# Weight conversion in a linear attention and two-MoE kernel: whole 32-bit words instead of 16-bit halves between ScalarE and VectorE

## The chip, the cores and the metric

The kernel runs on one core of a Trainium2 chip. The metric is the time of one execution on the device in microseconds (us). The kernel before took 1602.63 us (median of three runs, 1600.29 to 1602.99). Durations below come from one more execution that was profiled.

Five engines work side by side, each through its own queue of instructions in order: TensorE (PE, with PEld for its weight loads), VectorE (DVE), ScalarE (ACT), GpSimd (POOL) and SyncE (SP), which here only issues DMA transfers.

## The reference

Everything is float32. A linear attention (8 batches, 8 heads, 576 positions, 64 per head) is followed by two feed-forward blocks over 4608 tokens of 512 features:

```python
q_s = softmax(q, axis=-1); k_s = softmax(k, axis=2)
kv = einsum('bhsd,bhse->bhde', k_s, v)
x = einsum('bhsd,bhde->bhse', q_s, kv)        # reshaped to 4608 x 512
g = x @ w_gate                                 # 512 x 1536
y = (silu(g) * (x @ w_val)) @ w_out            # 1536 x 512
h = maximum(maximum(y @ w1, y @ w2), y @ w3)   # each 512 x 768
out = h @ w_out2                               # 768 x 512
```

## The kernel before

The weights reach the kernel as 64-bit floats: a weight tile of 128 x 512 numbers lies in a staging buffer as 128 x 1024 32-bit words, where word 0 of each pair is the low half of the double and word 1 the high half. The kernel makes float32 numbers of them itself ("conversion"), with two instructions on ScalarE and two on VectorE for each tile:

- `convert_act`: L486 reads the high words (one word in two) as floats, drops the sign, scales by a power of two and writes the result into the resident weight tile `plain`. L487 reads the low words as integers, scales them so that the upper three bits remain, and writes them as 16-bit integers. Their place is the lower half of the **high** word, so that L487 writes where L486 reads.
- `convert_dve`: L495 masks the high word in place, so that its sign bit and the three new bits remain (one source, one constant). L498 shifts `plain` left by three and merges the masked word into it.

There are 60 weight tiles to convert (12 each of `G`, `V` and `O` for the first block, 6 each of `W1`, `W2`, `W3` and `P` for the second). Each is converted once, in the first of nine token blocks (j = 0, 512 tokens each). `G`, `V` and `W1` to `W3` then stay in SBUF. `O` and `P` are written to DRAM as float32 and read again by every later block.

The matmuls take each float32 operand as two parts, `hi` (rounded, by a cast on ScalarE, L513) and `lo` (the rest, by a subtraction on VectorE, L518), and form three products (`mm3`, L524). Six tiles (`WHOLE`) are used as plain float32 (L554).

The work goes in groups of one weight tile each: `G`, `V`, `O`, ... and then `W1`, `W2`, `W3`, `P`, ... The loop over groups writes every engine's queue by hand, in this order: `convert_dve` of tiles that ScalarE has begun, `split_lo` for the group three ahead, `split_hi` for the group four ahead (L513), `convert_act` by a quota (about six groups ahead), the group's matmuls, steps of the attention for the next token block (`SLOTS`), and then `main_ev`, which takes the result out of PSUM: Silu on ScalarE (`s`, L587) for `G`, a product on VectorE (`h`, L590) for `V`, a copy on ScalarE (L594) for `W1`. Two PSUM banks serve these results in turn. The third and fourth results of the first block (`G1`, `V1`) lie in banks `acc0` and `acc1`, so the first accumulating matmul (L554, tile `O0`) can start only when L587 has emptied `acc0`, and its second quarter only when L590 has emptied `acc1`. A prologue (`PROLOGUE`) does the first half of the attention and the first six conversions.

Staging buffers are filled by SP: seven tiles ahead at first, three ahead after the 34th, since the first phase borrows space (`ring_yhi`, `ring_ylo`) that later holds `y`.

Of the kernel before, what the change touches and what calls it, by code (L numbers as in the profile page):

```python
# [11 lines left out]
U16 = mybir.dt.uint16  # L12
AF = mybir.ActivationFunctionType
ALU = mybir.AluOpType
# [4 lines left out]
def linear_attention_moe_moe_kernel(  # L19
# [20 lines left out]
    nc = tc.nc  # L40
# [45 lines left out]
    n, m = R * HH * D, HH * D  # L86
# [357 lines left out]
    staged = {}  # L444
# [28 lines left out]
    def convert_act(n):  # L473

        j, kind, f = groups[n]
        if kind in "OP":
            plain[n] = sb.tile([128, TB], F32, tag="plain", name="plain", bufs=3)  # L480
        else:
            plain[n] = resident(kind, f)
        words = staged[n].rearrange("p (n t) -> p n t", t=2)
        low, high = words[:, :, 0], words[:, :, 1]
        bits = staged[n].bitcast(U16).rearrange("p (n t) -> p n t", t=4)[:, :, 2]
        nc.scalar.activation(out=plain[n], in_=high.bitcast(F32), func=AF.Abs, scale=2.0 ** -112)  # L486
        nc.scalar.activation(  # L487
            out=bits, in_=low, func=AF.Copy, scale=2.0 ** -29 * (1.0 - 2.0 ** -7), bias=-0.44
        )

    def convert_dve(n):
        j, kind, f = groups[n]
        rest = staged.pop(n).rearrange("p (n t) -> p n t", t=2)[:, :, 1]
        wu = plain[n].bitcast(U32)
        nc.vector.tensor_scalar(  # L495
            out=rest, in0=rest, scalar1=0x80000007, scalar2=None, op0=ALU.bitwise_and
        )
        nc.vector.scalar_tensor_tensor(  # L498
            out=wu, in0=wu, scalar=3, in1=rest, op0=ALU.logical_shift_left, op1=ALU.bitwise_or
        )  # L500
        if kind in "OP":
            nc.sync.dma_start(out=kept[kind][f * 128:(f + 1) * 128, :], in_=plain[n])

    def resident(kind, f):
        return raw[kind][:, f].rearrange("p c f -> p (c f)")
# [176 lines left out]
    def converts_act(upto):  # L682
        while done["act"] < min(upto, GPB):
            loads(done["act"] + 1)
            convert_act(order[done["act"]])
            done["act"] += 1

    def converts_dve(upto):
        while done["dve"] < min(upto, GPB):
            convert_dve(order[done["dve"]])  # L690
            done["dve"] += 1
            n = done["dve"]
            loads(n + 7 if n + 7 <= RING else max(RING, n + 3))
# [168 lines left out]
```

## Time and profile before

| What | Value |
|---|---|
| median of three runs | 1602.63 us |
| the profiled execution | 1602.22 us |
| its span, first to last instruction | 1600.3 us |
| PE busy | 1549.9 us (97% of the span) |
| DVE busy | 951.9 us (59%) |
| ACT busy | 740.6 us (46%) |
| mean granted TensorE clock | 0.992 of full speed |

PE is busy almost throughout, and the shares of DVE and ACT are means over nine blocks of which only the first converts weights. The slices of the page show this: ACT is busy 9 tenths of the third and fourth slices of 40 us and 3 to 4 tenths from the seventh slice on; PE has 3 and 7 tenths in the first two slices and 9 in all others. What PE still loses must be looked for in the first 240 us, stretch by stretch. "Busy" counts an instruction from its start to its end; two successive instructions of ACT or DVE overlap a little, so the pace of a queue is read from start to start.

### The profile page before, as it was taken

To read this page: it belongs to the slowest core of one execution; us is meant where nothing else is said; L and a number is where in the kernel's file an instruction comes from. 1 tells how busy PE (TensorE), PEld (TensorE's weight loads), DVE (VectorE), ACT (ScalarE), POOL (GpSimd) and SP (SyncE) were. 2 spreads that over 40 slices of the span, in tenths; PEclk is the share of its full clock that TensorE was granted. 3 is DMA by queue.
4 is the path that set the end of the run, shared out by engine and by line. 5 is a ranking of instruction groups with operands and counts; after the bars stand their busy time and mean duration, and the time that the engine had idled before them with its cause. 6 is when DMAs were issued, how large, how long until landed. Compare 5 with 4: busy or idle time off the path is not lost.

```text
span 1600.3 us, 19611 instructions
## 1 busy us (share of the span) xinstructions
PE 1549.9 (97%) x7300; PEld 1266.1 (79%) x7300; DVE 951.9 (59%) x1622; ACT 740.6 (46%) x1234; POOL 23.5 (1%) x33
## 2 busy tenths in 40 slices
PE   3799999999999999999999999999999999999999
PEld 2487678888888888888888888888888888888887
DVE  7687885457554765367546754575547643664443
ACT  3799864344434443354335443444343433443332
POOL 1000000000000000000000000000000000000000
PEclk9899999999999999999999999999999999999999
DMA  7674744102310322120412141123103211111100
GB/s 191 192 230 148 206 119 109 34 24 66 96 37 23 70 73 57 33 63 30 99 33 48 36 109 34 30 60 95 38 22 70 66 34 40 34 53 32 29 26 33
DMA packets 197182, 112.95 MB, mean 71 GB/s; under 512 B 145888, under 2 KB 169440, under 8 KB 197088
## 3 DMA queue, kind: packets, MB, share of 16 engines
q1 hardware_dynamic: 192288, 110.54, 25.6%
q10 hardware_dynamic: 4800, 1.18, 0.4%
q8 instruction: 57, 0.93, 0.3%
q14 instruction: 37, 0.30, 0.1%
HBM read 97.52 MB, written 14.16 MB: 70 GB/s over the span
## 4 chain that ended last, share of the span: by engine, by line
PE 86%; ACT 7%; DVE 4%; issue 2%; DMA 1%; SPq 0%; DVEq 0%; ACTq 0%
PE pm L524 58%; PE acc L524 25%; ACT stage L487 2%; ACT whi L513 1%; PE pkv L254 1%; PE acc L554 1%; PE px L407 1%; PE px L406 1%; PE px L405 1%; DMA out_dram<-o 0%; ACT raw_w L486 0%; SPq L148 0%; ACT plain L486 0%; ACT ring_yhi L487 0%; DVE wlo L518 0%
## 5 line engine op out<-in xcount | busy, mean ns | idle before, releaser
L524 PE MATMUL pm<-xhi,whi 128*128 128x512 f32 x864 | 339.6, 393 | 8.8 <-ACT s L587 4.8
L524 PE MATMUL pm<-xhi,wlo 128*128 128x512 f32 x864 | 337.5, 391 | 0.2 <-DVE wlo L518 0.2
L524 PE MATMUL pm<-xlo,whi 128*128 128x512 f32 x864 | 337.4, 390 | 0.0
L590 DVE TENSOR_TENSOR h<-s,pm 128x512 f32<-128x512 f32 x108 | 74.2, 687 | 334.3 <-PE pm L524 332.0
L524 PE MATMUL pm<-yhi,whi 128*128 128x512 f32 x648 | 255.2, 394 | 4.6 <-ACT s L594 4.3
L524 PE MATMUL pm<-ylo,whi 128*128 128x512 f32 x648 | 253.2, 391 | 0.2 <-DVE ylo L608 0.2
L524 PE MATMUL pm<-yhi,wlo 128*128 128x512 f32 x648 | 252.8, 390 | 0.0
L544 ACT CAST hhi<-h 128x512 fp32r<-128x512 f32 x156 | 97.3, 624 | 317.7 <-DVE h L590 209.7
L524 PEld LDWEIGHTS pm<-xhi,whi 128*128 128x128 f32 x864 | 162.8, 188 | 46.4 <-ACT s L587 6.9
L524 PEld LDWEIGHTS pm<-xhi,wlo 128*128 128x128 f32 x864 | 162.8, 188 | 35.3 <-DVE wlo L518 1.3
L524 PEld LDWEIGHTS pm<-xlo,whi 128*128 128x128 f32 x864 | 162.9, 189 | 34.1 <-issue 0.7
L524 PE MATMUL acc<-hhi,whi 128*128 128x512 f32 x424 | 165.0, 389 | 0.0
L524 PE MATMUL acc<-hhi,wlo 128*128 128x512 f32 x424 | 164.9, 389 | 0.0
L524 PE MATMUL acc<-hlo,whi 128*128 128x512 f32 x424 | 164.9, 389 | 0.0
L587 ACT ACTIVATE s<-pm 128x512 f32<-128x512 f32 x108 | 65.4, 605 | 180.7 <-PE pm L524 180.5
L524 PEld LDWEIGHTS pm<-yhi,whi 128*128 128x128 f32 x648 | 121.9, 188 | 33.3 <-ACT s L594 5.5
L524 PEld LDWEIGHTS pm<-yhi,wlo 128*128 128x128 f32 x648 | 122.1, 188 | 25.8
L524 PEld LDWEIGHTS pm<-ylo,whi 128*128 128x128 f32 x648 | 121.9, 188 | 25.2 <-DVE ylo L608 0.5
L513 ACT CAST whi<-raw_w 128x512 fp32r<-128x512 f32 x162 | 100.8, 622 | 56.5 <-PE pm L524 43.1
L518 DVE TENSOR_TENSOR wlo<-plain,whi 128x512 fp32r<-128x512 f32 x156 | 106.9, 685 | 17.1 <-ACT whi L513 17.0
L518 DVE TENSOR_TENSOR wlo<-raw_w,whi 128x512 fp32r<-128x512 f32 x162 | 109.9, 683 | 10.2 <-ACT whi L513 10.2
L545 DVE TENSOR_TENSOR hlo<-h,hhi 128x512 fp32r<-128x512 f32 x156 | 107.9, 692 | 12.5 <-ACT hhi L544 0.7
(149 smaller groups left out, 1959.1 us busy)
## 6 DMA issues: line engine op xcount, KB each, us to landing
plain<-kept_o SPq DMA_DIRECT2D x96, 256.0 KB, 2.6
plain<-kept_p SPq DMA_DIRECT2D x48, 256.0 KB, 2.8
out_dram<-o SPq DMA_DIRECT2D x36, 256.0 KB, 2.0
stage<-in_moe_w_dram SPq DMA_DIRECT2D x17, 512.0 KB, 3.9
k_sb<-in_k_dram SPq DMA_DIRECT2D x56, 128.0 KB, 3.3
v_sb<-in_v_dram SPq DMA_DIRECT2D x56, 128.0 KB, 2.8
stage<-in_moe_w_out_dram SPq DMA_DIRECT2D x12, 512.0 KB, 4.3
stage<-in_moe_w_gate_dram SPq DMA_DIRECT2D x6, 512.0 KB, 4.8
```

The lines of the kernel that those rows point to most:

```text
L254: nc.tensor.matmul(out=c["pkv"][u * D:(u + 1) * D, g, :], lhsT=lhsT, rhs=rhs, start=i == 0, stop=i == R,)
L405: nc.tensor.matmul(out=px[:, a:e], lhsT=hi, rhs=qhi, start=True, stop=False)
L406: nc.tensor.matmul(out=px[:, a:e], lhsT=hi, rhs=qlo, start=False, stop=False)
L407: nc.tensor.matmul(out=px[:, a:e], lhsT=lo, rhs=qhi, start=False, stop=True)
L487: nc.scalar.activation(out=bits, in_=low, func=AF.Copy, scale=2.0 ** -29 * (1.0 - 2.0 ** -7), bias=-0.44)
L513: nc.scalar.copy(out=hi, in_=plain[n])
L518: nc.vector.tensor_tensor(out=lo, in0=plain.pop(n), in1=hi, op=ALU.subtract)
L524: nc.tensor.matmul(out=o, lhsT=a, rhs=b, start=first and m == 0, stop=last and m == 2)
L544: nc.scalar.copy(out=hi, in_=h)
L545: later.append(lambda: nc.vector.tensor_tensor(out=lo, in0=h, in1=hi, op=ALU.subtract))
L587: nc.scalar.activation(out=st["s"], in_=p, func=AF.Silu)
L590: nc.vector.tensor_tensor(out=h, in0=st["s"], in1=p, op=ALU.mult)
```

## The change

L487 now writes its three bits as a whole 32-bit integer over the **low** word that it has read, and no longer as 16 bits into the high word. On VectorE the mask of one source becomes an operation with two sources: the high word is masked to its sign bit and merged with the low word in one instruction. The number of instructions on each engine stays the same, and so does their order. The new lines are one or two lines further up in the file (L486 becomes L484, L487 becomes L485, L495 becomes L494, L498 becomes L497, L513 becomes L512).

```diff
         words = staged[n].rearrange("p (n t) -> p n t", t=2)
         low, high = words[:, :, 0], words[:, :, 1]
-        bits = staged[n].bitcast(U16).rearrange("p (n t) -> p n t", t=4)[:, :, 2]
         nc.scalar.activation(out=plain[n], in_=high.bitcast(F32), func=AF.Abs, scale=2.0 ** -112)
         nc.scalar.activation(
-            out=bits, in_=low, func=AF.Copy, scale=2.0 ** -29 * (1.0 - 2.0 ** -7), bias=-0.44
+            out=low, in_=low, func=AF.Copy, scale=2.0 ** -29 * (1.0 - 2.0 ** -7), bias=-0.44
         )
 
     def convert_dve(n):
         j, kind, f = groups[n]
-        rest = staged.pop(n).rearrange("p (n t) -> p n t", t=2)[:, :, 1]
+        words = staged.pop(n).rearrange("p (n t) -> p n t", t=2)
+        low, rest = words[:, :, 0], words[:, :, 1]
         wu = plain[n].bitcast(U32)
-        nc.vector.tensor_scalar(
-            out=rest, in0=rest, scalar1=0x80000007, scalar2=None, op0=ALU.bitwise_and
+        nc.vector.scalar_tensor_tensor(
+            out=rest, in0=rest, scalar=0x80000000, in1=low, op0=ALU.bitwise_and, op1=ALU.bitwise_or
         )
```

What moves is a wait. On ScalarE's queue in the prologue, at the fourth to seventh conversions, the rows before stood as follows; `Activation_49` is the semaphore that ScalarE's own instructions raise, `DVE_49` and `PE_49` those of VectorE and TensorE, and `DMAHW` those of transfers:

```order
L486 ACTIVATE plain<-ring_yhi 128x512 [waits DMAHW6_49]
L487 ACTIVATE ring_yhi<-ring_yhi 128x512 [waits Activation_49]
L486 ACTIVATE raw_g<-ring_ylo 128x512 [waits DMAHW7_49]
L487 ACTIVATE ring_ylo<-ring_ylo 128x512 [waits Activation_49]
L486 ACTIVATE raw_v<-ring_ylo 128x512 [waits DMAHW0_49]
L487 ACTIVATE ring_ylo<-ring_ylo 128x512 [waits Activation_49]
```

And the same place in the changed kernel:

```order
L484 ACTIVATE plain<-ring_yhi 128x512 [waits DMAHW6_49]
L485 ACTIVATE ring_yhi<-ring_yhi 128x512
L484 ACTIVATE raw_g<-ring_ylo 128x512 [waits DMAHW7_49]
L485 ACTIVATE ring_ylo<-ring_ylo 128x512
L484 ACTIVATE raw_v<-ring_ylo 128x512 [waits DMAHW0_49]
L485 ACTIVATE ring_ylo<-ring_ylo 128x512
```

Before, all 60 instructions of L487 wait for the end of the L486 just ahead of them, because they write into words that it reads. In the changed kernel none does: 27 of the 60 still name ScalarE's own semaphore, but for an instruction at least eight places further back. VectorE's queue has one instruction replaced by another at each conversion, with the same waits.

## Rows read from the trace of the kernel before

**Rows 1.** Windows: us, busy us (count) of PE, PEld, DVE, ACT, POOL; PEclk, DMA share, GB/s

```profile
41.60:72.00 30.40, 21.98 (x57) 12.82 (x58) 17.98 (x31) 25.13 (x34) 0.00 (x0) 0.80 0.62 174
72.00:137.00 65.00, 65.00 (x286) 53.16 (x284) 52.28 (x94) 61.32 (x85) 1.15 (x1) 1.00 0.67 204
137.00:200.00 63.00, 57.01 (x251) 41.38 (x251) 48.33 (x86) 55.83 (x76) 1.28 (x1) 0.97 0.67 199
200.00:231.00 31.00, 28.24 (x142) 20.65 (x141) 26.19 (x49) 25.59 (x38) 0.00 (x0) 0.94 0.49 139
231.00:1600.30 1369.30, 1364.37 (x6464) 1129.15 (x6462) 777.98 (x1300) 557.51 (x982) 16.34 (x12) 1.00 0.20 51
```

**Rows 2.** Timeline of PE: start, us, instruction, [idle before, what ended it]

```profile
64.61 6.87 PE L554 MATMUL acc<-h,plain 128*128 128x512 f32 x8 [5.43 <-DVE stage L495]
...
149.11 0.67 PE L524 MATMUL pm<-xhi,whi 128*128 128x512 f32 x1 [3.39 <-ACT s L587]
...
178.85 0.50 PE L524 MATMUL pm<-yhi,whi 128*128 128x512 f32 x1 [1.51 <-ACT s L594]
...
223.41 0.50 PE L524 MATMUL pm<-yhi,whi 128*128 128x512 f32 x1 [1.98 <-ACT s L594]
```

**Rows 3.** Windows after three of those stalls: us, PE busy us (count), PEclk, DMA, GB/s

```profile
64.60:71.40 6.80, 6.79 (x9) 0.55 0.99 219
149.10:152.50 3.40, 3.39 (x8) 0.53 0.67 218
224.50:227.80 3.30, 3.30 (x9) 0.50 0.03 11
```

**Rows 4.** Timeline of ACT in the prologue: start, us, instruction

```profile
53.46 0.70 ACT L486 ACTIVATE raw_g<-ring_ylo 128x512 f32<-128x512 f32 x1
54.20 1.38 ACT L487 ACTIVATE ring_ylo<-ring_ylo 128x512 uint16<-128x512 uint32 x1
55.32 0.70 ACT L486 ACTIVATE raw_v<-ring_ylo 128x512 f32<-128x512 f32 x1
...
63.88 0.68 ACT L587 ACTIVATE s<-pm 128x512 f32<-128x512 f32 x1
64.46 0.60 ACT L513 CAST whi<-plain 128x512 fp32r<-128x512 f32 x1
```

**Rows 5.** Windows, instructions of L487 alone: us, ACT busy (count), PEclk, DMA, GB/s

```profile
51.00:65.00 14.00, 6.78 (x5) 0.96 0.61 191
72.00:137.00 65.00, 30.51 (x23) 1.00 0.67 204
```

**Rows 6.** Groups by line: shapes, xcount | busy us, mean ns of one | idle before

```profile
L487 ACT ACTIVATE stage<-stage 128x512 uint16<-128x512 uint32 x41 | 55.9, 1362 | 1.3
L486 ACT ACTIVATE raw_w<-stage 128x512 f32<-128x512 f32 x17 | 11.5, 679 | 2.1 <-DMA stage<-in_moe_w_dram 2.1
L495 DVE TENSOR_SCALAR stage<-stage 128x512 uint32<-128x512 uint32 x41 | 17.5, 427 | 20.6 <-ACT stage L487 20.4
L498 DVE SCALAR_TENSOR_TENSOR raw_w<-raw_w,stage 128x512 uint32<-128x512 uint32 x17 | 11.8, 693 | 0.6
L518 DVE TENSOR_TENSOR wlo<-raw_w,whi 128x512 fp32r<-128x512 f32 x162 | 109.9, 683 | 10.2 <-ACT whi L513 10.2
```

**Rows 7.** Timeline of DVE, two places: start, us, instruction

```profile
65.84 0.68 DVE L590 TENSOR_TENSOR h<-s,pm 128x512 f32<-128x512 f32 x1
...
103.51 0.68 DVE L590 TENSOR_TENSOR h<-s,pm 128x512 f32<-128x512 f32 x1
104.11 0.42 DVE L495 TENSOR_SCALAR stage<-stage 128x512 uint32<-128x512 uint32 x1
104.57 0.69 DVE L498 SCALAR_TENSOR_TENSOR raw_v<-raw_v,stage 128x512 uint32<-128x512 uint32 x1
```

**Rows 8.** Waits, of DVE (40 to 225 us) and ACT (60 to 225): us, times, longest

```profile
DVE stage L495 <- ACT stage L487: 18.3, 21, 2.1
ACT plain L486 <- DMA stage<-in_moe_w_out_dram: 4.5, 1, 4.5
```

## The prediction

> **What bounds the kernel now.** I read the windows by stretch first, since the shares of the whole span average nine token blocks of which only the first converts weights. From 231 us on PE is busy 1364.4 of 1369.3 us: nothing is to be had there. In the first block it lacks 8.4 us of 30.4 (41.6 to 72), nothing of 65 (72 to 137), 6.0 of 63 and 2.8 of 31 [rows 1]. So 17.2 us of idle time lie in reach of a change to the conversion; what PE lacks before 41.6 us is mostly softmax. The second view is PE's timeline at these stalls: 5.43 us before 64.61, 3.39 before 149.11, 1.51 before 178.85, 1.98 before 223.41, and three end on a ScalarE instruction that empties a PSUM bank [rows 2]. The first names L495, but the matmul there needs bank acc0, which L587 empties from 63.88 to 64.56, so it is ScalarE's too [rows 4]. Third, the clock after a stall: in the stretches after the first, second and fourth the granted clock is 0.55, 0.53 and 0.50, that is 1.2 GHz instead of 2.4 [rows 3]. A stall thus costs its idle time and then half of the stretch behind it: 3.4, 1.6 and 1.65 us.
>
> Who makes ScalarE late is seen in the same windows: ACT is busy 61.3 of 65 us and 55.8 of 63, DVE 52.3 and 48.3 [rows 1]. L487 has 30.5 us of the 61.3 [rows 5], at 1362 ns each where L486, of the same size, takes 679 [rows 6].
>
> **The change on ScalarE.** Today a conversion takes ACT's queue 1.86 us from start to start (53.46 to 55.32): 0.74 for L486, whose end L487 awaits, and 1.12 for L487 [rows 4]. Two things change. First the wait goes; the old L486 will overlap its successor as other instructions do, which follow each other after about 0.58 (63.88 to 64.46) [rows 4]. So 0.74 becomes 0.58. Second, L487 writes 32-bit words. The trace has no ScalarE instruction that writes every second word, so I bound its duration: not below 0.60 us, the cast L513 [rows 4], and not above the 1.36 us of today [rows 6]. L486 reads every second word, and differs from L487 in its output (packed words, not 16 bits in every fourth half-word) and in the input's type. I take L486's 0.68, the nearest row, as I put the excess on the 16-bit writes. Its pace is then 0.58 too. A conversion comes to 1.16 us and gives back 0.70; if only the wait goes, 0.16.
>
> **The change on VectorE.** L495 (427 ns, the next start 0.46 after its own: 104.11 to 104.57 [rows 7]) becomes an instruction with two sources. Below, it can't be faster than 427; the nearest row is L498, also with two sources, one of them every second word: 693 ns, against 683 for L518, whose operands all lie packed [rows 6]. A step of one word thus costs next to nothing in a read, and L495 reads and writes in such steps in 427. I take 0.69 and a step of 0.72 (L498 must still wait for its end): +0.26 per conversion. The upper bound is 1.36, the longest time that a conversion instruction has in these rows. With 23 conversions in 72 to 137 [rows 5] VectorE goes from 52.3 to 58.3 us of 65. It has that room: it stood waiting for L487 for 18.3 us at L495 alone [rows 8], and that wait shortens.
>
> Against this stands a rule of the Trainium skill (Vector Engine (DVE) Microarchitecture Reference, section 5.2, measured stream behaviour): a port keeps its full rate only for runs of at least two neighbouring words, and one that steps at every element takes 1.71 to 2.51 ns per column. By it the new instruction would take an estimated 0.95 to 1.36 us. The rows don't bear it out for a step of two words, since L495 takes 427 ns in just that pattern [rows 6]; it stays as the mechanism of a rival below.
>
> **The sum,** along the four stalls.
>
> - Up to 71.5 us. Two conversions of the prologue stand on the chain, each 0.70 less 0.26: -0.9. Between 51 and 65 us ScalarE does five conversions in a row [rows 5]: 5 x 0.70 = 3.5 of the 5.43 us stall. So L554 starts at 60.2 instead of 64.61. Its second quarter needs acc1, which L590 empties; L590 started 1.96 us after L587 (65.84 [rows 7] after 63.88), with VectorE's conversion and L518 between, and two conversions add 0.5. It starts at 59.5 + 1.96 + 0.5 = 62.0 and ends 0.68 later. Three quarters remain: 0.86 us each at full clock or 1.72 at half (6.87 for four [rows 2]). They end at 65.2 or 67.8 instead of 71.48: -6.3 or -3.7. The remaining idle time (about 1.9, then 1.6) is near that of the fourth stall, after which the half clock lasted 3.3 us and cost 1.65 [rows 3]; with that: -4.7.
> - 149.11: ScalarE is behind by what piled up since 72 us. 23 conversions x 0.70 = 16 us is far more than 3.39. The stall goes, and its 1.6 of half clock: -5.0.
> - 178.85: likewise, -1.5.
> - 223.41: the chain of waits behind it begins with a load of q for the next block, which needs a buffer that VectorE frees, and runs through 16 issues on SP's queue, the transfer and VectorE's maximum; two conversions are in it. The change moves these by about 1 us only. All of it would be -1.98 - 1.65 = -3.6; I take -2, with 0 and -3.6 as ends.
>
> Sum: -4.7 - 5.0 - 1.5 - 2.0 = -13.2. The profiled execution took 1602.22 (its span 1600.3 and 1.9 around it; the median of the runs is 1602.63, 0.4 more), so I forecast 1589.0. Ends of this case: -3.7 - 5.0 - 0 - 0 = -8.7 and -6.3 - 5.0 - 1.5 - 3.6 = -16.4, or 1585.8 to 1593.5. What the edits cost elsewhere is hidden by PE's own work: in 72 to 137 us it has no idle time at all [rows 1], and VectorE's extra 6 us run beside it.
>
> **Rivals.**
>
> (a) The write was not the cause. If L487 is slow through its stepped, in-place access or its integer input, only the wait goes. Five conversions give 0.8 where 5.43 are lost, and the prologue's two lose 0.1 each: -0.6, half clock as before. At 149.11, 23 x 0.16 = 3.7 still covers 3.39: -5.0. Nothing certain behind that: 1602.2 - 5.6 = 1596.6. For it: nothing in the trace isolates the 16-bit write. Against it: L486 steps in its read and takes half the time. The Trainium skill has a rule on this side too (SBUF — State Buffer, the passage on SBUF cachelines): two hits on a line of 16 bytes suffice for the full rate, whatever is hit. By it both forms, with a step of 8 bytes, would run alike, and the result would be this rival's.
>
> (b) VectorE's merge is the new bound, and the kernel gets slower. Its place is 72 to 231 us. VectorE has 65 - 52.3 = 12.7 us free in 72 to 137, and some 0.09 per instruction by overlap (693 ns against a step of 0.60, 103.51 to 104.11 [rows 7]) x 94 = 8.5: 21 us for 23 conversions, 0.92 each. It decides from an instruction of about 1.35 us on; in 137 to 231, where the waits for q are VectorE's own, somewhat earlier. At 1.36 the step is 1.39, +0.93 per conversion: 1.9 on the prologue's two, little in 72 to 137, and in 137 to 231 74.5 us of work less 12 of overlap plus 25 x 0.93 = 86 of 94, of which PE today idles 8.8; allowing 2 for the wait on q, about 3 are lost. With nothing gained, 1602 + 5 = 1607. Against it: rows 6, above.
>
> (c) The transfers keep the pace. A faster conversion asks sooner for staged tiles, of which only three are in flight after the 34th; ScalarE has already waited 4.5 us once for one [rows 8], when SP's queue was full of loads of q. Then the later stalls come back as waits for tiles and only the first term holds: 1602.2 - 4.7 = 1597.5. Against it: the DMA engines are busy 0.67 in 72 to 200 us and 0.49 after [rows 1].
>
> **Chances.** Forecast 0.66, (a) 0.19, (b) 0.06, (c) 0.09. What a measurement can tell from no change is 0.2%, 3.2 us, so "faster" means below 1599.4. The forecast counts fully, (a) with 0.16 and (c) with 0.06: 0.88; same 0.06, slower 0.06. The range goes from 1585 to 1598 and leaves out (b), parts of (a) and (c), and a clock that recovers better than I reckon. The forecast's own range is 1586 to 1593.5.
>
> **What would show it.** Right: the instruction at the new L485 near 0.68 us, its predecessor followed after 0.6 rather than 0.74; the new L494 near 0.69; ACT busy in 72 to 137 us down by some 16 us; no stall near 140 to 150 us; the stall before L554 under 2.5 us. L485 at 1.3 is (a); L494 above 1.2 with PE waiting on VectorE is (b); ACT waiting for staged tiles by more than 8 us in all is (c). The forecast is wrong if PE still idles more than 8 us between 41 and 231 us, or if new stalls arise in later blocks, which I exclude since no instruction there changes.

## The result

The changed kernel took 1585.65 us (median of four runs, 1585.37 to 1585.97), the kernel before on the same chip 1601.99 (four runs, 1600.29 to 1602.99): a ratio of 0.9899, 95% interval 0.9882 to 0.9916. The forecast was 1589.0 with a range of 1585 to 1598; the result lies 0.65 us inside the lower end of that range, and just outside the ends of the forecast's own sum (1585.8 to 1593.5). The profiled execution took 1585.46 us, its span 1583.5, so the 1.9 us around the span are as before and the gain in the trace is 16.8 us.

The windows of the changed kernel, in the columns of [rows 1]:

```profile
41.60:72.00 30.40, 25.02 (x86) 16.78 (x85) 24.18 (x37) 21.34 (x38) 0.00 (x0) 0.92 0.71 200
72.00:137.00 65.00, 65.00 (x288) 53.82 (x287) 61.92 (x103) 52.78 (x95) 1.42 (x1) 1.00 0.73 229
137.00:200.00 63.00, 61.23 (x292) 44.26 (x290) 55.78 (x94) 42.14 (x75) 1.06 (x1) 1.00 0.68 193
200.00:231.00 31.00, 29.70 (x141) 22.65 (x142) 27.42 (x50) 17.51 (x34) 0.00 (x0) 1.00 0.31 103
231.00:1583.50 1352.50, 1347.53 (x6393) 1116.35 (x6391) 765.14 (x1276) 552.03 (x972) 16.36 (x12) 1.00 0.20 51
```

PE now lacks 5.4, 0, 1.8 and 1.3 us where it lacked 8.4, 0, 6.0 and 2.8. The granted clock is 1.00 in the second to fourth stretch, where it was 1.00, 0.97 and 0.94. Between 72 and 137 us the two helpers have changed places: ACT fell from 61.3 to 52.8 us and VectorE rose from 52.3 to 61.9 of 65. Its waits turned with it. DVE's between 40 and 231 us (line waited for: us, times, longest):

```profile
DVE stage L494 <- ACT stage L485: 3.0, 5, 0.9
DVE xlo L418 <- ACT xhi L417: 2.8, 2, 1.9
```

VectorE waited for ScalarE's conversion for 18.3 us on `stage` alone [rows 8]; 3.0 are left. ScalarE now waits for VectorE, for `h` by 10.8 us, where it had been 1.2, and longer for staged tiles (ACT's waits between 40 and 230 us):

```profile
ACT hhi L543 <- DVE h L589: 10.8, 9, 2.4
ACT plain L484 <- DMA stage<-in_moe_w_out_dram: 7.0, 4, 5.8
ACT raw_w L484 <- DMA stage<-in_moe_w_dram: 6.2, 5, 3.4
```

The groups of the two changed instructions, against L487 and L495 in [rows 6]:

```profile
L485 ACT ACTIVATE stage<-stage 128x512 uint32<-128x512 uint32 x41 | 27.3, 665 | 0.0
L494 DVE SCALAR_TENSOR_TENSOR stage<-stage 128x512 uint32<-128x512 uint32 x41 | 28.2, 687 | 4.7 <-ACT stage L485 4.3
```

1362 ns became 665, and 427 became 687. ScalarE's queue at the place of [rows 4]:

```profile
50.98 0.65 ACT L485 ACTIVATE ring_yhi<-ring_yhi 128x512 uint32<-128x512 uint32 x1
51.53 0.68 ACT L484 ACTIVATE raw_g<-ring_ylo 128x512 f32<-128x512 f32 x1
52.11 0.66 ACT L485 ACTIVATE ring_ylo<-ring_ylo 128x512 uint32<-128x512 uint32 x1
52.67 0.67 ACT L484 ACTIVATE raw_v<-ring_ylo 128x512 f32<-128x512 f32 x1
```

From one L484 to the next (51.53 to 52.67) a conversion takes 1.14 us of the queue; it took 1.86.

PE's stalls, as in [rows 2]:

```profile
59.60 1.13 PE L553 MATMUL acc<-h,plain 128*128 128x512 f32 x2 [1.68 <-ACT s L586]
62.08 2.84 PE L553 MATMUL acc<-h,plain 128*128 128x512 f32 x6 [1.35 <-DVE h L589]
...
199.91 0.50 PE L523 MATMUL pm<-yhi,whi 128*128 128x512 f32 x1 [0.93 <-DVE s L595]
207.62 0.50 PE L523 MATMUL pm<-yhi,whi 128*128 128x512 f32 x1 [0.96 <-ACT s L593]
```

The stall of 5.43 us is now two, 1.68 and 1.35. That of 149.11 and that of 178.85 are gone; the one of 223.41 is the 0.96 at 207.62. The 0.93 before 199.91, which ends on VectorE, is new. And the clock did not fall after any of them. Windows after L553's stalls:

```profile
59.50:64.40 4.90, 3.44 (x9) 1.42 (x9) 4.83 (x8) 4.04 (x9) 0.00 (x0) 1.00 1.03 270
64.40:68.00 3.60, 3.60 (x17) 2.80 (x16) 3.39 (x5) 1.86 (x4) 0.00 (x0) 1.00 0.89 178
```

In [rows 3] the same place ran at a mean of 0.55, most of it at the lower level of 1.2 GHz; here it is 2.4 GHz throughout, after two shorter stalls with matmuls between them.

Where the gain arises is seen by following the same instruction through both traces. First PE after the eight L554/L553, before and then after (start, us, instruction):

```profile
70.92 0.80 PE L524 MATMUL pm<-xhi,whi 128*128 128x512 f32 x1
```

```profile
64.36 0.79 PE L523 MATMUL pm<-xhi,whi 128*128 128x512 f32 x1
```

That is 6.6 us. The matmul of 149.11 [rows 2] starts at 138.22 (10.9), the first `pkv` matmul of the next block's attention, at 181.79 before, at 166.23 (15.6), that of 223.41 at 207.62 (15.8), and the one after the half clock of that stall, 227.87 before, at 210.47 (17.4). The first block's output then leaves, on SP's queue, before and after:

```profile
245.27 4.44 SPq L624 DMA_DIRECT2D out_dram<-o  x4
```

```profile
228.45 4.44 SPq L623 DMA_DIRECT2D out_dram<-o  x4
```

16.8 us, the difference of the spans (1600.3 less 1583.5). The eight later blocks neither add nor take anything.

### The profile page after: what moved, and what is told of

Same layout as the page of the kernel before. It is cut to its first block, busy times and chain, and to the rows that moved or that the text cites. A ratio compares the mean times of both kernels' runs of the same rounds, so it can differ in the third digit from the quotient of the medians.

```text
span 1583.5 us, 19634 instructions
## 1 busy us (share of the span) xinstructions
PE 1542.3 (97%) x7300; PEld 1263.2 (80%) x7300; DVE 964.6 (61%) x1622; ACT 699.6 (44%) x1234; POOL 23.6 (1%) x33
## 4 chain that ended last, share of the span: by engine, by line
PE 91%; DVE 4%; DMA 1%; ACT 1%; issue 1%; SPq 0%; DVEq 0%; ACTq 0%
PE pm L523 62%; PE acc L523 26%; PE pkv L254 1%; PE acc L553 1%; DVE wlo L517 1%; DVE stage L494 1%; DMA stage<-in_moe_w_dram 1%; PE px L406 1%; DMA out_dram<-o 1%; PE px L407 1%; PE px L405 0%; SPq L148 0%; DMA raw_w<-in_k_dram 0%; DVE raw_w L497 0%; DVE s L595 0%
## 5 line engine op out<-in xcount | busy, mean ns | idle before, releaser
L589 DVE TENSOR_TENSOR h<-s,pm 128x512 f32<-128x512 f32 x108 | 74.2, 687 | 333.1 <-PE pm L523 330.8
L586 ACT ACTIVATE s<-pm 128x512 f32<-128x512 f32 x108 | 64.5, 597 | 180.9 <-PE pm L523 180.8
L512 ACT CAST whi<-raw_w 128x512 fp32r<-128x512 f32 x162 | 100.2, 619 | 57.7 <-PE pm L523 43.1
L517 DVE TENSOR_TENSOR wlo<-plain,whi 128x512 fp32r<-128x512 f32 x156 | 106.8, 684 | 17.4 <-ACT whi L512 17.3
```

Of the source, the lines that this page charges most:

```text
L512: nc.scalar.copy(out=hi, in_=plain[n])
L517: nc.vector.tensor_tensor(out=lo, in0=plain.pop(n), in1=hi, op=ALU.subtract)
L586: nc.scalar.activation(out=st["s"], in_=p, func=AF.Silu)
L589: nc.vector.tensor_tensor(out=h, in0=st["s"], in1=p, op=ALU.mult)
```

## The experiments

All times are medians in us, each beside runs of the kernel before on the same chip (1601.01 for e1 to e4, 1601.78 for e5 to e7, 1601.64 for e8 and e9, 1601.28 for e10 and e11). "First output" is the start of the row just shown, in the profiled execution of each kernel. The medians of the kernel before differ by up to 1 us between these groups, so two variants from different groups are better compared by their ratios. e1, e2, e7 and e8 leave out the signs and the true low bits of the weights, e4 the three low bits; the others do the full computation.

| Kernel | Time | Ratio to before, 95% interval | First output |
|---|---|---|---|
| before | 1601.99 | | 245.3 |
| after | 1585.65 | 0.9899 (0.9882 to 0.9916) | 228.5 |
| e1: 16 bits into the low word, no wait | 1600.52 | 0.9997 (0.9988 to 1.0006) | 246.0 |
| e2: 32-bit words, wait back | 1587.21 | 0.9915 (0.9900 to 0.9929) | 231.1 |
| e3: only VectorE's two sources | 1605.92 | 1.0028 (1.0016 to 1.0039) | 251.2 |
| e4: after, VectorE with one source | 1581.15 | 0.9878 (0.9864 to 0.9893) | 224.9 |
| e5: after, merge done twice | 1619.76 | 1.0111 (1.0094 to 1.0128) | 263.1 |
| e6: after, conversions one later | 1619.48 | 1.0112 (1.0097 to 1.0127) | 263.1 |
| e7: 16 bits, packed, wait back | 1588.86 | 0.9918 (0.9903 to 0.9933) | 229.0 |
| e8: 16 bits, one per word, wait back | 1588.58 (one run) | | 231.4 |
| e9: after, conversions one earlier | 1602.06 | 1.0007 (0.9998 to 1.0015) | 245.5 |
| e10: after, q loaded by GpSimd | 1588.55 | 0.9918 (0.9905 to 0.9932) | 232.7 |
| e11: e9, q loaded by GpSimd | 1600.31 | 0.9992 (0.9983 to 1.0001) | 241.3 |

The time of the profiled execution less its first output is 1355.7 to 1357.5 us in every row: this is a contest about the first token block alone. (The profiled executions are not the medians. e1's took 1603.16 us, e3's 1607.77, e7's 1585.95, the shortest of its four, and e11's 1597.93, so the last two columns need not move together between close rows.)

### Which half of ScalarE's change paid (e1, e2, e7, e8)

**e1** keeps the narrow write but moves it to the low word, so that nothing overlaps L486's read. VectorE has the new two-source form.

```diff
+        bits = staged[n].bitcast(U16).rearrange("p (n t) -> p n t", t=4)[:, :, 0]
-            out=low, in_=low, func=AF.Copy, ...
+            out=bits, in_=low, func=AF.Copy, ...
-            out=rest, in0=rest, scalar=0x80000000, in1=low, op0=ALU.bitwise_and, op1=ALU.bitwise_or
+            out=rest, in0=low, scalar=7, in1=rest, op0=ALU.bitwise_and, op1=ALU.bitwise_and
```

> As the changed kernel, but ScalarE writes its three bits as 16-bit halves into the low word that it has read (not into the high word): the wait for L484 is gone as in the changed kernel, the write is as narrow as before. VectorE keeps two sources of the same pattern; sign and low bits of the weights come out wrong. Theory W (the narrow write made L487 slow): the instruction takes 1.36 us again, a conversion 1.7 us of ScalarE's queue, time 1594 to 1598, half clock after the stall before L553. Rival A (the wait, the step or the integer input made it slow): 0.67 us and 1585 to 1588.

**e2** writes whole words, but over the high word, so that the wait is back:

```diff
-            out=low, in_=low, func=AF.Copy, ...
+            out=high, in_=low, func=AF.Copy, ...
-            out=rest, in0=rest, scalar=0x80000000, in1=low, op0=ALU.bitwise_and, op1=ALU.bitwise_or
+            out=rest, in0=rest, scalar=7, in1=low, op0=ALU.bitwise_and, op1=ALU.bitwise_and
```

> As the changed kernel, but ScalarE's 32-bit words go over the high words, so that the wait for the end of L484 is back in all 60 conversions. VectorE has two sources of the same pattern; the sign is lost. Theory W: 0.66 us for the instruction, 0.72 + 0.56 = 1.28 us per conversion, so 0.12 to 0.16 more than the changed kernel; the stall before L553 grows by 0.6 to 0.8 us to about 2.4, time 1586 to 1589, the upper end if the clock falls to half there. Rival A, in the form that the wait is what counted: most of the gain is lost, 1594 or more.

ScalarE's groups, first e1, then e2 (these kernels' line numbers differ by one):

```profile
L486 ACT ACTIVATE stage<-stage 128x512 uint16<-128x512 uint32 x41 | 55.6, 1356 | 0.0
```

```profile
L485 ACT ACTIVATE stage<-stage 128x512 uint32<-128x512 uint32 x41 | 27.9, 681 | 1.3
```

Without any wait the narrow write still takes 1356 ns; with the wait the word takes 681. So at this step of 8 bytes the width of the write made L487 long, and the wait did not. Each kernel has VectorE's two-source form, so e3 (below), which has it with the narrow write and the wait, is their common base: the width alone is worth 18.7 us (1605.92 to 1587.21), the wait 5.4 us while the write is narrow (1605.92 to 1600.52) and about 2 once it is wide (e2's ratio is 0.9915, after's 0.9899; the intervals overlap, so this is the weakest of the three). By the traces e2's first output is 2.6 us later than the changed kernel's, and 1.7 us of that arise where the clock falls behind L553, which it does in e2 and not in the changed kernel. I had expected e1 to gain at least 3 us on the kernel before; it gained nothing that can be told from zero, since VectorE's price (e3) equals what the wait returned.

**e7** and **e8** ask what it is in a narrow write. Both write 16 bits again, with e2's wait and VectorE work; in e7 the results lie next to each other, in e8 there is one in each 32-bit word, both in the first half of the tile.

```diff
+        bits = staged[n].bitcast(U16)[:, 0:TB]                                          # e7
+        bits = staged[n].bitcast(U16).rearrange("p (n t) -> p n t", t=2)[:, 0:TB, 0]    # e8
-            out=low, in_=low, func=AF.Copy, ...
+            out=bits, in_=low, func=AF.Copy, ...
```

> ScalarE's second instruction writes 16-bit integers again, but next to each other, into the first quarter of the staged tile; the wait for its predecessor is back, and VectorE's mask and merge have the changed kernel's sources and lengths (low weight bits are not the reference's). If it is the step between 16-bit writes (one half-word in four) that took 1362 ns, this write takes 0.60 to 0.70 us and the kernel 1585.5 to 1589, as e2. If any conversion to 16 bits takes twice as long on this engine, it takes 1.3 to 1.4 us and the kernel loses ScalarE's gain while VectorE's dearer merge stays: 1603 to 1607, as e3.

> As e7, but the 16-bit integers lie one to a 32-bit word (every second half-word), still in the first half of the staged tile (low weight bits are not the reference's). e7's packed halves took 671 ns, before's one half-word in four 1362 ns. If a write of half a word is what costs, as long as its other half is not written next, this takes 1.3 to 1.4 us and the kernel 1600 to 1607, as e3 without ScalarE's gain. If it is the step of 8 bytes together with 16 bits, or any step above some size, it takes 0.65 to 1.0 us and the kernel 1586 to 1595.

The groups, e7 and then e8:

```profile
L486 ACT ACTIVATE stage<-stage 128x512 uint16<-128x512 uint32 x41 | 27.5, 671 | 1.3
```

```profile
L486 ACT ACTIVATE stage<-stage 128x512 uint16<-128x512 uint32 x41 | 32.5, 792 | 1.3
```

Conversion to 16 bits costs nothing (671 ns packed, 665 for 32-bit words), half a word at a time costs a little (792), and only the old pattern, two bytes in every eight, costs double. e8's first alternative (1.3 to 1.4 us for any half word) is out. What in the engine makes it so, no run shows. e7's time is that of e2 within the intervals, as it should be if the write's duration is all that matters.

### What VectorE's dearer instruction costs (e3, e4, e5)

**e3** is the kernel before with its mask as a two-source instruction and nothing else; **e4** is the changed kernel with a one-source mask; **e5** is the changed kernel with L494 issued twice.

```diff
 # e3, on the kernel before
-        nc.vector.tensor_scalar(
-            out=rest, in0=rest, scalar1=0x80000007, scalar2=None, op0=ALU.bitwise_and
+        nc.vector.scalar_tensor_tensor(
+            out=rest, in0=rest, scalar=0x80000007, in1=rest, op0=ALU.bitwise_and, op1=ALU.bitwise_and
 # e4, on the changed kernel
-        nc.vector.scalar_tensor_tensor(
-            out=rest, in0=rest, scalar=0x80000000, in1=low, op0=ALU.bitwise_and, op1=ALU.bitwise_or
+        nc.vector.tensor_scalar(
+            out=rest, in0=rest, scalar1=0x80000000, scalar2=None, op0=ALU.bitwise_and
 # e5, on the changed kernel
+        nc.vector.scalar_tensor_tensor(
+            out=rest, in0=rest, scalar=0x80000000, in1=low, op0=ALU.bitwise_and, op1=ALU.bitwise_or
+        )
```

> The kernel before with VectorE's part of the change alone: the masking of the high word is done as an operation with two sources (the same words twice), so each conversion costs VectorE 0.26 us more and ScalarE gains nothing. Theory W: VectorE waits for ScalarE anyway and takes it out of that wait; only the two conversions on the prologue's chain show, 0.5 us each at most: 1602 to 1604. Rival B (VectorE was near its limit): 60 x 0.26 = 15 us, a good part of it seen, 1607 or more.

> The changed kernel with VectorE's masking of one source as before (427 ns); the three low bits are left out of the weights. Theory W: about 0.3 us at each of the two conversions on the prologue's chain and 0.5 at the second bank, and some of the small stalls after 180 us: 1583 to 1585.3. Rival B (VectorE is the bound of the changed kernel): 23 x 0.26 = 6 us and more, 1580 or below.

> VectorE does the merge (L494) twice, so a conversion costs it 0.72 us more and the merge together 1.41 us, just past the 1.35 us from which rival (b) let VectorE decide. If VectorE's time counts in proportion, as e3 and e4 suggest (4.5 to 4.9 us for 0.26 us), 0.72 us costs some 12 to 14 us on the changed kernel's 1585.6: 1597 to 1600. Rival (b) as it was priced, with none of ScalarE's gain left: about 1607. If VectorE had the room that the prediction gave it, next to nothing: up to 1588.

e3's mask takes 691 ns and the kernel 4.9 us more than before (1605.92 less 1601.01); e4's takes 423 and the kernel 4.5 less than after (1581.15 against 1585.65). By the ratios to the kernel before, e4 gains 3.4 us on the changed kernel rather than 4.5, and the two intervals touch; by the first outputs it is 3.6. e3's interval is 2.6 to 6.2 us. The same 0.26 us per conversion thus costs some 3.4 to 4.9 us in either setting, and without it ScalarE's part of the change is worth 19.9 us (1601.01 less 1581.15). In both kernels the time fell between the two cases that I had named: VectorE is neither free nor the bound. The stalls of e4 show where:

```profile
60.67 2.84 PE L553 MATMUL acc<-h,plain 128*128 128x512 f32 x6 [0.80 <-DVE h L589]
...
196.98 0.50 PE L523 MATMUL pm<-yhi,whi 128*128 128x512 f32 x1 [0.60 <-DVE s L595]
204.66 0.50 PE L523 MATMUL pm<-yhi,whi 128*128 128x512 f32 x1 [0.97 <-ACT s L593]
```

L553 starts at 58.75, not 59.60, with no wait before it: L586 is 0.85 us earlier, and the matmuls ahead end later, at a granted clock of 0.59 from 52.0 to 55.3 us (1.00 in the changed kernel). The wait for L589 is 0.80, not 1.35. By its next matmul (62.95, against 64.36) e4 leads by 1.4 us. At the matmul of 163.42 (162.30 in e4) it leads by 1.1: in between, where the changed kernel's PE has no idle time, VectorE's dearer work cost next to nothing. The rest of the lead is won after that, where PE waits on what VectorE delivers. The first such place is the attention of the next block, the changed kernel and then e4:

```profile
183.43 0.36 PE L405 MATMUL px<-qthi,kvhi 128*128 128x256 f32 x1 [0.56 <-ACT qthi L389]
```

```profile
181.33 0.68 PE L405 MATMUL px<-qthi,kvhi 128*128 128x256 f32 x1
```

`qthi` is ScalarE's, but ScalarE had waited for VectorE's transpose there (`whole`, L388, 2.4 us in two waits). The lead is 2.1 us here, 2.9 at 199.91 and 3.6 at the first output (224.88). The remaining 1 us lies in later blocks, where the instructions are the same, and may be no more than scatter. In e3, where ScalarE is still full, it is different: e3 falls 1.5 us behind the kernel before between 71 and 149 us.

In e5 the price is 34 us for 0.72 us per conversion, not the 12 to 14 of proportion. Two windows of e5, as above:

```profile
72.00:137.00 65.00, 60.26 (x253) 47.83 (x252) 63.46 (x103) 42.02 (x76) 1.41 (x1) 0.97 0.66 195
137.00:200.00 63.00, 56.84 (x253) 41.24 (x252) 60.94 (x99) 45.33 (x77) 0.00 (x0) 0.97 0.59 174
```

VectorE is busy 63.5 of 65 us and 60.9 of 63: it is full, PE idles 4.7 and 6.2 us, and the clock falls after its stalls (0.97). So VectorE decides when the merge takes 1.41 us in all, just past the 1.35 us that rival (b) named as the turning point. Where between 0.69 and 1.41 us it turns, no run shows; with VectorE at 61.9 of 65 us the changed kernel may be close to it.

### Moving the conversions (e6, e9), and the queue behind them (e10, e11)

`LEAD` says by how many groups the quota of `convert_act` (how many conversions ScalarE has to have done) runs ahead.

```diff
-LEAD = 6
+LEAD = 5        # e6; in e9 and e11 LEAD = 7
```

> The changed kernel with the quota of conversions one lower (LEAD = 5, not 6), so that one conversion fewer stands ahead of the first L586 on ScalarE and of the first L589 on VectorE. If the remaining stall before L553 (1.1 and 2.8 us of idle PE) is what those conversions make, it shrinks by 1 to 2 us and the kernel takes 1583.5 to 1585. If the conversions that are put off are missed later instead, the stall comes back there: 1585.5 to 1590. If L589 waits for something else, no change: 1585.5.

> The changed kernel with the quota of conversions one higher (LEAD = 7, not 6). Before the first L586 one conversion more stands on both engines: the stall before L553 grows by 1.2 to 1.9 us. In e6, one fewer cost 34 us, as every L512 then waited for the L497 just issued. If the changed kernel still waits a little for that reason (L512 waits for L497 by 11.6 us in all), one more lead takes those waits away, and the late stalls (183 to 226 us, 2.6 us) go: 1583 to 1586. If the lead of six is enough, only the earlier stall is left: 1586.5 to 1589. If the staged tiles cannot come so early, ScalarE waits for transfers ahead of urgent work: 1589 to 1600.

Both came out slower than any case that I had named (at most 1590 and 1600): 34 and 16 us above the changed kernel. e6 did so for a reason that I had not listed. Its waits of ACT between 40 and 225 us:

```profile
ACT whi L512 <- DVE raw_v L497: 23.2, 11, 4.4
ACT whi L512 <- DVE raw_w L497: 14.0, 8, 3.1
ACT whi L512 <- DVE plain L497: 10.5, 9, 1.6
ACT whi L512 <- DVE raw_g L497: 9.5, 9, 1.1
```

57 us in 37 waits; in the changed kernel the four come to 11.6. With one group less of lead, L512 asks for a tile whose L497 VectorE has not finished yet, at most of the groups of the first block, and all that stands behind L512 on ScalarE's queue waits too, the emptying of PSUM (L586) among it. PE waits for that by 11.5 us in six pieces, beside the one before L553. In e9 it is a staged tile. PE's two longest stalls in e9, and ScalarE's instructions before them:

```profile
183.80 0.79 PE L523 MATMUL pm<-yhi,whi 128*128 128x512 f32 x1 [3.73 <-ACT s L593]
209.83 0.80 PE L523 MATMUL pm<-yhi,whi 128*128 128x512 f32 x1 [7.62 <-ACT s L593]
```

```profile
181.44 0.66 ACT L484 ACTIVATE plain<-stage 128x512 f32<-128x512 f32 x1 [7.39 <-DMA stage<-in_moe_w_out_dram]
207.10 0.66 ACT L484 ACTIVATE plain<-stage 128x512 f32<-128x512 f32 x1 [7.14 <-DMA stage<-in_moe_w_out_dram]
```

And SP's queue in e9 (start, us until the last issue, line, count):

```profile
170.57 2.02 SPq L120 DMA_DIRECT2D k_sb<-in_k_dram  x4
...
177.10 0.53 SPq L463 DMA_DIRECT2D stage<-in_moe_w_out_dram  x1
...
193.26 10.01 SPq L148 DMA_DIRECT2D q_sb<-in_q_dram  x16
203.38 0.41 SPq L463 DMA_DIRECT2D stage<-in_moe_w_out_dram  x1
```

The tile for which ScalarE waits until 207.10 was asked for at 203.38, behind 16 loads of q; the one for 181.44 at 177.10, behind the loads of k and v. Hence e10 and e11, which hand the loads of q to GpSimd's queue:

```diff
-                        nc.sync.dma_start(out=t["qp"][p:p + 32, g, s0 // 32:s1 // 32], in_=a[u, e, g])
+                        nc.gpsimd.dma_start(out=t["qp"][p:p + 32, g, s0 // 32:s1 // 32], in_=a[u, e, g])
```

> The changed kernel with the loads of q (L148, 16 issues in 10.5 us on SP's queue in the first block, from 182.7 us) issued by GpSimd instead, so that the loads of staged tiles behind them leave up to 10 us sooner. If the changed kernel's remaining wait of ScalarE for a staged tile (5.8 us at 198.4) and the small stalls at 200 to 208 us come from that queue, they go: 1582.5 to 1585. If that wait was hidden anyway: 1585 to 1586. If GpSimd issues so slowly or its transfers disturb the others so that q comes late, slower: 1587 to 1600, with waits of VectorE for q in every block.

> e9 (LEAD = 7, 1602.1 us) with the loads of q issued by GpSimd. e9's longest stall (7.6 us at 209.8) follows a staged tile whose load was issued at 203.4, right behind 16 loads of q. If that queue is what takes e9's gain, as rival (c) would have it, the stall and its half clock go and the time is 1586 to 1593. If the order of work on ScalarE and VectorE makes e9 slow and the tile only shows it, little changes: 1599 to 1603.

In e11 the second stall fell from 7.62 to 2.72 us, and the tile's load left at 198.43 instead of 203.38, but the time fell by 1.8 us only (the first output by 4.2). The stall behind the loads of k and v stayed (3.76 us at 182.18), and a stretch at half clock came in: 0.50 from 192.4 to 199.0 us, after a stall of 2.28 us at L405, where e9 has 1.00 after one of 2.42. In e10 the longest wait for a tile went from 5.8 to 3.3 us and the kernel became 2.9 us slower, the third of its cases: VectorE's maximum now waits 4.74 us for q where it had waited 1.4, and PE stalls for 4.19 us at 203.42. So q is what must not be late. Whether the changed kernel's wait for tiles costs anything e10 can't tell, since q's delay lies at the same place; the only stall of PE behind it that ends on ScalarE is the 0.96 us before 207.62.

By the starts of the same matmuls e9 loses 3.3 us against the changed kernel at L553 (2.79 us of idle time, then half clock), 5.3 at the first of its two long stalls and the half clock behind it, 2.0 at L405, 9.5 at the second long stall and its half clock, and gets 3.0 back before the first output. So the two stalls behind staged tiles hold 14.8 of 17.1 us. That the queue order is a part of it is shown, by the 4.9 us of e11; that it is the greater part is not.

No version tried beats the changed kernel with the full computation; e4, the only faster one, leaves out three bits of every weight.

## Why the prediction was right, and where its sizes were off

The mechanism held on ScalarE's side and in where the gain arises; that the time came within 3.4 us of the forecast is in part luck, as misses of opposite sign met. **ScalarE:** 0.68 us forecast for L485, 0.665 measured; 1.16 per conversion, 1.14. **VectorE:** 0.69 forecast for the instruction, 0.687; 58.3 us of 65 in 72 to 137 us, 61.9 measured, as nine more of its instructions fall there (103, not 94). The rule of the Trainium skill that was weighed there (Vector Engine (DVE) Microarchitecture Reference, section 5.2) gave an estimated 0.95 to 1.36 us; the measured 0.687 decides against it for steps of two words. The Trainium skill's rule on cachelines (SBUF — State Buffer, the passage on SBUF cachelines) would have had both widths alike; 1356 ns (e1) against 665 ns at the same step of 8 bytes decides against it here.

**The sum.** Forecast 13.2 us, measured 16.8. By the starts in the result:

- Up to L554's end: forecast -4.7 (ends -3.7 and -6.3), measured -6.6. This is the largest miss. The matmul started at 59.60 (forecast 60.2) and its second bank at 62.08 (forecast 62.7, the end of an L590 that starts at 62.0), so the stalls were right to 0.6 us; what failed is the half clock after them, which the sum took as likely. The remaining idle time came in two pieces, and the granted clock stayed at 1.00. e2 shows the other side of that edge: there the first piece is 2.37 us, not 1.68, the granted clock is 0.62 from 63.1 to 67.6 us, and the six matmuls behind the second take 4.54 us instead of 2.84.
- 149.11: forecast -5.0. The matmuls from 70.92 to the stall gained little, and 10.9 less 6.6 us is 4.3 at its start; the half clock that ended at 152.5 [rows 3] adds 1.6. Together -5.9; some 0.8 of it was won before the stall.
- 178.85: forecast -1.5. From the 12.5 us so far to 15.6 at 181.79, about -3. The sum had left out two small stalls of the kernel before at 162.9 and 163.7 (0.35 and 0.22 us of idle time and slower matmuls), which went too, 1.1 us in all.
- 223.41: forecast -2. It gained 1.8 by 227.87, as the half clock there went, and 0.6 of that was returned before the output left. -1.2, within its ends of 0 and -3.6.

**"What the edits cost elsewhere is hidden by PE's own work"** is the step that was wrong in kind. In 72 to 137 us it held for the changed kernel: PE is busy for 65.00 of 65 us, and e4's lead does not grow there. But the sum drew from this one window that VectorE's dearer instruction costs nothing anywhere behind the prologue, and from 163 us on PE does wait on what VectorE delivers. e3 and e4 price the whole at some 3.4 to 4.9 us, of which the sum had about 1 (0.5 us at the prologue's two conversions, as much ahead of L590). The forecast came out near because the clock after L553 and two uncounted stalls gave back as much and more. That is luck: in e2, where L553's first stall is 0.7 us longer, the clock did fall.

**The signs.** No stall near 140 to 150, L553's idle time 1.68 and 1.35: right, though I had named one stall under 2.5. PE idles 8.5 us between 41.6 and 231 where more than 8 was to refute the forecast. By its letter this sign speaks against the forecast, but the limit contradicted the forecast's own sum, which takes at most 1.9, 3.39, 1.51 and 1.98 us off the 17.2 and so leaves at least 8.4. The idle time fell by 8.7 us from 17.2, and most of the rest of the gain is stretches that no longer run at half clock. ACT's busy time in 72 to 137 us fell by 8.5 us, not 16: L485 itself fell from 30.5 to 16.05 us, but ScalarE, no longer behind, did ten instructions more in the window (95, not 85). The sign was badly chosen, the mechanism not.

**The rivals.** (a), only the wait: refuted by 665 ns, and by e1. Its price for the wait alone, 5.6 us, agrees with e1 against e3 (5.4) by luck. It put 5.0 of them on the stall of 149.11, and in e1 this stall stands, with half clock behind it (0.50 from 149.3 to 152.7 us):

```profile
148.75 0.50 PE L524 MATMUL pm<-xhi,whi 128*128 128x512 f32 x1 [3.38 <-ACT s L587]
```

So 23 conversions that are each 0.16 us shorter on ScalarE's queue do not cover it, though (a) reckoned that they would. The largest piece of e1's gain on e3 lies near 163 us, where e3 stalls for 1.75 us before a matmul with `yhi` and e1 does not. (b), VectorE as the bound: not at 0.69 us, but e5 shows it at the doubled merge, dearer than worked out (+18 us over before instead of +5). ScalarE waits for VectorE's results by 51 us in e5 (33 in the changed kernel) and passes the delay on, and the clock, which (b) left out, is 0.90 from 200 to 264 us; how much of the excess is each, no run separates. (c), the transfers: its sign was met, since ScalarE waited for tiles by 13.2 us in all where 8 were named, yet at most the 0.96 us before 207.62 followed on PE. In e9 it happened.

## What to carry to other kernels

Look at the output's pattern, not only its size: an instruction that takes twice as long as its sibling of the same shape may owe it to short writes with wide gaps. When work is moved from a full engine to one with room, test the price on the receiving engine by itself (the old kernel with only the dearer instruction), since "not full" is not "free": a window in which the busiest engine has no gap says nothing of the windows behind it. A hand-set lead is tuned to the instruction durations on both sides: here one group less or more cost 34 and 16 us.

## What was not expected of the hardware

- On ScalarE, a 128 x 512 conversion from every second 32-bit word takes 665 ns into every second word, 671 into packed halves, 792 into one half of each word, and 1356 to 1366 into one half in every two words. The Trainium skill (ScalarE: Activation LUTs, What ACT_TABLE_LOAD costs) gives 186 ns plus 0.833 ns per element for an instruction with constants, whatever the function, which is an estimated 613 ns here. The first two rows are near it, the last is not.
- After L553's stalls of 1.68 and 1.35 us the granted clock stayed at 1.00; after 2.37 and 1.20 at the same place (e2) it was 0.62 from 63.1 to 67.6 us, and the next six matmuls took 4.54 us instead of 2.84.
- GpSimd issued the 16 loads of q about as fast as SP (183.4 to 193.8 us in e10, 182.7 to 193.2 in the changed kernel), but they landed later after their issue (median 3.3 us, longest 5.9, against 2.0 and 3.9), and VectorE's wait for q rose from 1.4 to 4.74 us.
